# Chunk scan, gated unit and squared-ReLU unit on one core: how C is spread over its heads, what the first tokens are read from, and which steps go first

## Chip, cores and metric

One core of one Trainium2 chip runs the whole program. The metric is device microseconds of one execution; the median over several executions counts. TensorE is PE in the profile, its weight loads PEld, VectorE is DVE, ScalarE is ACT, GpSimd is POOL, and SyncE, whose queue issues the DMAs, is SP.

## The reference

Three stages follow each other, all in float32.

The scan takes 4 batches of 8 heads, 768 tokens each, 32 values per token and head and a state of 16. It is a linear recurrence, written in chunks:

```
L = exp(cum_i - cum_j) for j <= i              # cum: running sum of log(clip(a))
y_intra = ((C B^T) * L) x                      # inside a chunk
y_inter = (C state) * exp(cum)                 # from the chunks before
state   = decay_full * state + sum(decay_from_j * B x)
```

Its 3072 x 256 output goes through a gated unit, `silu(x w_gate) * (x w_val) w_out` with 1536 hidden columns (called GLU below), and that one's output through `relu(x w_in)^2 w_out` with 2048 hidden columns.

## The kernel before, in words

Every operation is put into a graph with an engine, a modelled cost, its dependencies, a priority (a smaller number goes first) and the buffers that it takes. `Graph.order` simulates the engines with these costs and writes out one order for all; each engine then works through its own instructions strictly in that order. So a priority or a modelled cost is not followed at run time, but fixes what stands ahead of what on each queue, SP's DMA issues included.

The scan runs in 28 chunks of up to 112 tokens, seven for each batch (`chunk_ops`). Chunk k needs the state of chunk k-1: the PE product `ys` (L668) gives outputs and state, ACT copies the state out (L702), PE turns it (L707) and ACT puts it into the next chunk's operand (L710). A chunk also needs its decays, scanned on DVE (L600 for chunk 0 and all late chunks, two halves at L570 for chunks 1 to 6), scores on PE (`cb`, L630), and their product on DVE (L654, two per chunk). The seven chunks of batch 0 are the early ones. Their B and C come by DMA: B into `eb` (L461), C into `ec` (L471), a 128 x 4 x 128 tile of zeros into which two DMAs put each head in a place of its own. PE transposes B once (L479) and the four slabs of C (L481), ACT copies both out (L485, L488). A POOL product (L614) makes the state columns; it reads `eb`, and only after it may the DMA of the next but one chunk write there.

Each weight comes as float64 words in units of two DMAs (L379). ACT (L394, L388) and DVE (L400, L405, L409) make float32 of a unit. A split then makes two float32r parts of it, `hi` on ACT (L415) and `lo` on POOL (L420). There are nine units for the GLU (six `gv`, gate and value columns, and three `o`), eight for the last stage.

A GLU step takes one block of 128 hidden columns over some tokens. An exact step multiplies the float32 tokens `xf` with the unconverted unit, two matmuls for each product; a step in parts takes the products of `xh_all`, `xl_all` with `hi`, `lo`, six matmuls each. Gate and value columns are made by PE (L736), then tanh on ACT (L799), two products on DVE (L802, L805), in parts also a copy on ACT (L821) and the rest on POOL (L826), then the output product on PE (L853). Batch 0 has two tiles, 336 and 432 tokens, whose GLU steps are cut into the cells of `PLAN["cells"]` (pair of blocks, first and last chunk, exact or not); the other six tiles run in order, 72 steps. For the early chunks all seven outputs go into `xf` first (L683); two large copies (L723, L726) then make their parts once all chunks of a tile are there. In the GLU the DVE operations have a priority of 3000 less than the rest of their step (a step's is 10000 or more, an early chunk's or unit's below 3600).

The last stage (`relu2`) has 6 tiles of 512 tokens by 16 blocks. Each of the 96 steps has a front of 6 matmuls (L736), ReLU on ACT (L904), a square on DVE (L907), a copy on ACT (L910), a rest on DVE (L914), and a back of 12 matmuls (L926). When a tile is done, ACT copies one half of its sum and DVE the other (L949, L951), and SP stores both (L954).

PSUM has 8 banks here (`ps=8`). Each of the two first GLU tiles holds two for its sums from its first output product to its end.

Of the kernel before, what the change touches and what calls it, by code (L numbers as in the profile page):

```python
# [34 lines left out]
class Graph:  # L35
# [14 lines left out]
    def order(self):  # L50
        for op in self.ops:
            op.wait = len(op.deps)
            for d in op.deps:
                d.next.append(op)
        avail, out, events, now = {}, [], [], 0.0
# [6 lines left out]
        while left:  # L62
            started = True
            while started:
                started = False
                for eng, ops in avail.items():
# [4 lines left out]
                    for op in ops:  # L71
                        if best is not None and op.prio > best.prio:
                            continue
                        need.clear()
                        for b in op.bufs:
                            if not b.taken:
                                need[b.pool] = need.get(b.pool, 0) + 1
                        if op.keep and "ps" in need:
                            need["ps"] += op.keep()
                        if all(self.pools[p] >= k for p, k in need.items()):  # L80
                            best = op
                    if best is None:
                        continue
                    ops.remove(best)
                    for b in best.bufs:
                        if not b.taken:
                            b.taken = True
                            self.pools[b.pool] -= 1
                    best.start = now
# [8 lines left out]
                    heapq.heappush(events, (now + best.cost, seq, 0, best))  # L98
                    started = True
            if not events:  # L100
                raise RuntimeError("the operations wait for each other: " + str(
                    {e: [(o.eng, o.prio, getattr(o.fn, "__qualname__", "")[-30:], [b.pool for b in o.bufs if not b.taken]) for o in v][:6] for e, v in avail.items()}))
            now = events[0][0]
            while events and events[0][0] <= now:
                _, _, kind, op = heapq.heappop(events)
                if kind == 0:
                    busy[op.eng] = None
                    left -= 1
                    for b in op.bufs:
                        b.left -= 1  # L110
                        if not b.left:
                            self.pools[b.pool] += 1
# [14 lines left out]
def kernel(  # L127
# [64 lines left out]
    eb = [const.tile([P, P], F32, name=f"eb{i}") for i in range(NEB)]  # L192
    ec = [const.tile([P, G, P], F32, name=f"ec{i}") for i in range(NEB)]
# [76 lines left out]
    def setup_eb(i):  # L270

        nc.gpsimd.memset(ec[i], 0.0)
        nc.gpsimd.memset(eb[i][0:NS], 0.0)
        v = eb[i][0:NS].rearrange("p (h n) -> p h n", h=H)
# [3 lines left out]
        )  # L278

# [31 lines left out]
    op_eb = [g.add("POOL", 1100, lambda i=i: setup_eb(i), prio=-999 + 10 * i) for i in range(NEB)]  # L311
# [114 lines left out]
    ck = [Chunk() for _ in range(NK)]  # L426

    def chunk_ops(k, prio, after=(), load_after=()):
# [27 lines left out]
        if early:  # L456
            e = Buf(f"eb{k % NEB}")
            c.bt, psb, psc = Buf("tr"), Buf("ps"), Buf("ps")

            def load_b():  # L460
                nc.sync.dma_start(  # L461
                    out=eb[k % NEB][NS : NS + n].rearrange("p (h n) -> p h n", h=H),
                    in_=B[b, :, t : t + n, :].rearrange("h t n -> t h n"),
                )

            def load_c():
                z = ec[k % NEB]
                for u in range(HG):
                    v = z[NS : NS + n, :, u * 64 : u * 64 + 64].rearrange("p w (s n) -> p w s n", s=G)
                    v = bass.AP(v.tensor, v.offset, [list(v.ap[0]), [P + NS, G], [1, NS]])  # L470
                    nc.sync.dma_start(out=v, in_=C[b, u * G : (u + 1) * G, t : t + n, :].rearrange("h t n -> t h n"))  # L471

            lb = dma("SP", 1, 480, 650, load_b, [op_eb[k % NEB], *load_after], ldp, [e])
            lc = dma("SP", 2, 480, 650, load_c, [op_eb[k % NEB], *load_after], ldp, [e])

            def transpose():
                pb = new(psb, [P, P], F32, "trb")
                pc = new(psc, [P, G, P], F32, "trc")
                nc.tensor.transpose(pb, eb[k % NEB], eye)  # L479
                for w in range(G):  # L480
                    nc.tensor.transpose(pc[:, w], ec[k % NEB][:, w], eye)  # L481

            def copy_b():
                c.bt.t = tt = new(c.bt, [P, 1 + G, P], F32, "bct")
                nc.scalar.activation(tt[:, 0], psb.t, AF.Copy)  # L485
# [5 lines left out]
            o = g.add("PE", 800, transpose, [lb, lc, op_eye, before.tr if before else None], prio, [e, psb, psc, c.bt], lat=250)  # L491
            o1 = g.add("ACT", 300, copy_b, [o], prio, [psb, c.bt])
            c.tr = g.add("ACT", 570, copy_c, [o1], prio, [psc, c.bt])
# [118 lines left out]
        def state_columns():  # L612
            v = eb[k % NEB].rearrange("p (h n) -> p h n", h=H) if early else bc[k % NBC][:, 0]
# [65 lines left out]
        if early:  # L679
# [6 lines left out]
        else:  # L686
            def keep_h():
                nc.scalar.activation(xh_all[:, :, dd], yv()[:, :, :n], AF.Copy)

            def keep_l():  # L690
                nc.vector.tensor_tensor(
                    xl_all[:, :, dd], yv()[:, :, :n], xh_all[:, :, dd].bitcast(F32), op=ALU.subtract
                )

            o1 = g.add("ACT", 360, keep_h, [o], prio - 5, [psy])
            c.x = g.add("DVE", 390, keep_l, [o1], prio - 5, [psy])
# [22 lines left out]
    def in_parts(o, n, prio, deps):  # L719
        d = slice(o, o + n)  # L720

        def high():
            nc.scalar.activation(xh_all[:, :, d], xf_buf.t[:, :, d], AF.Copy)  # L723

        def rest():
            nc.vector.tensor_tensor(  # L726
                xl_all[:, :, d], xf_buf.t[:, :, d], xh_all[:, :, d].bitcast(F32), op=ALU.subtract
            )

        h = g.add("ACT", 230 + 1.67 * n, high, deps, prio, [xf_buf])  # L730
        return g.add("DVE", 170 + 2.1 * n, rest, [h], prio, [xf_buf], port=True)


# [11 lines left out]
    W1, W2 = {}, {}  # L745

    def glu(tl, f, o, n, exact, prio, deps, pool_rest=True):
# [60 lines left out]
        a1 = g.add("ACT", 180 + el, tanh, [o1] if wide else [o1, o2], prio, [pg, tb])  # L808
        a2 = g.add("DVE", 160 + 1.04 * n, gate, [a1], prio - 3000, [pg, tb], lat=60)
        a3 = g.add("DVE", 160 + 1.04 * n, times, [a2, o2], prio - 3000, [pg, pv, tb] if wide else [pg, tb])  # L810
# [5 lines left out]
        else:  # L816
# [11 lines left out]
            a4 = g.add("ACT", 200 + el, high, [a3], prio, [tb, pb])  # L828
# [58 lines left out]
    def relu2(i, f, prio, deps):  # L887
# [47 lines left out]
        o1 = g.add("PE", 6 * 232, front, [u.parts, *deps], prio, [ph, u.hi, u.lo], lat=260)  # L935
        o1.keep = lambda: 0 if ab[0].taken else 2
        o = g.add("ACT", 600, relu, [o1], prio, [ph, tb])
        o = g.add("DVE", 690, square, [o], prio - 3000, [tb])
        o = g.add("ACT", 625, high, [o], prio, [tb, pb])
        o = g.add("DVE" if late else "POOL", 690 if late else 1300, rest, [o], prio - (3000 if late else 0), [tb, pb])  # L940
        bk = g.add("PE", 12 * 120, back, [o], prio, [*ab, pb, u.hi, u.lo], lat=260)
        if f == NF2 - 1:
            for m in range(2):
                ob = Buf("tmp")

                def drain(m=m, ob=ob):
                    ov = new(ob, [P, 512], F32, "o")
                    if m == 0:
                        nc.scalar.activation(ov, acc[-1 - i][m], AF.Copy)  # L949
                    else:  # L950
                        nc.vector.tensor_copy(ov, acc[-1 - i][m])  # L951

                def store(m=m, ob=ob):
                    nc.sync.dma_start(  # L954
                        out=out[t0 + m * 256 : t0 + (m + 1) * 256, :].rearrange("(i p) f -> p i f", p=P),
                        in_=ob.t.rearrange("p (i f) -> p i f", i=2),
                    )

                o = g.add("ACT" if m == 0 else "DVE", 690, drain, [bk], prio - 3000, [ab[m], ob])
                dma("SP", 1, 480, 700, store, [o], prio, [ob])  # L960
# [16 lines left out]
    for u, at in zip(units, PLAN["split_at"]):  # L977
        W1[u].split(abs(at) * 100, "POOL", [last_unit] if at < 0 else [])
    xparts = [
        in_parts(o, n, at * 100, [ck[k].xf for k in ks])  # L980
        for (o, n, ks), at in zip(((0, cut, range(3)), (cut, S - cut, range(3, NCB))), PLAN["xparts_at"])
    ]
    for i, (j, c0, c1, exact) in enumerate(PLAN["cells"]):
        ti, o = (0, c0 * Q) if c0 < 3 else (1, c0 * Q - cut)
        n = min(c1 * Q, S) - c0 * Q
        for f in (2 * j, 2 * j + 1):
            deps = [ck[k].xf for k in range(c0, c1)] if exact else [xparts[ti]]
# [51 lines left out]
    with tc.manual_schedule():  # L1039
# [10 lines left out]
    xparts_at=[0.1, 5.59],  # L1050
    cells=[
        (0, 3, 7, 0),
        (2, 1, 3, 1),
        (3, 3, 7, 0),
        (0, 0, 3, 0),
        (2, 0, 1, 1),
        (2, 3, 7, 0),
        (4, 3, 7, 0),
        (5, 0, 3, 0),
        (3, 0, 3, 1),  # L1060
        (5, 3, 7, 0),
        (1, 5, 7, 1),
        (1, 3, 5, 0),
        (4, 0, 3, 0),
        (1, 0, 3, 0),
    ],
    pace=[-3, 2.73, 1],
    second=[52, 4, 6],
# [31 lines left out]
```

## Time and profile before

| | before |
|---|---|
| median of 3 runs | 692.1 us (690.78 to 692.5) |
| profiled execution | 690.22 us |
| span of its trace | 688.4 us |
| PE busy | 643.6 us, 93% of the span |
| DVE busy | 414.9 us, 60% |
| ACT busy | 328.2 us, 48% |
| POOL busy | 230.5 us, 33% |
| mean granted TensorE clock | 0.984 |

The span runs from the first to the last instruction; the profiled execution took 1.8 us more than that, and the median of the runs lies 1.9 us above the profiled execution. A stretch's idle time of an engine is its length less the busy time. The granted clock is a share of 2.4 GHz.

### The profile page before, as it was taken

The page shows a single profiled execution, that of the slowest core. Times are in us where ns is not written, and L with a number is a line of the kernel's source. Part 1 is how long each engine was busy: PE and PEld are TensorE (multiplying, and loading weights), DVE is VectorE, ACT ScalarE, POOL GpSimd, SP SyncE. Part 2 cuts the span into 40 slices and gives each one's busy share as a digit, 9 for nine tenths or more (in the row PEclk, how much of TensorE's full clock was granted, in tenths as well). Part 3 has the DMA queues.
Part 4 walks back from the last instruction along what each step waited for, and adds up shares of the span by engine and source line. Part 5 has one row for each costly group of instructions (what it writes and reads, how often), then busy time and mean ns, then how long its engine had stood idle before and what let it go on. Part 6 is the DMA issues. An engine that isn't in the chain of part 4 may idle for free.

```text
span 688.4 us, 11170 instructions
## 1 busy us (share of the span) xinstructions
PE 643.6 (93%) x4339; PEld 583.0 (85%) x4339; DVE 414.9 (60%) x588; ACT 328.2 (48%) x641; POOL 230.5 (33%) x228
## 2 busy tenths in 40 slices
PE   2567999999999999999999998999999999999996
PEld 1455788999998899888999977898989999998985
DVE  6999965347666664756566797545363535353533
ACT  6467454244454544544556664435353534343432
POOL 5244667336756654566355571000000000000000
PEclk9986999999999999999999999999999999999998
DMA  7768721504565576643432310000000000000000
GB/s 229 179 163 203 151 63 44 98 2 78 105 136 107 80 129 119 134 73 69 153 106 80 119 65 1 0 31 1 1 32 1 3 29 1 31 1 1 31 0 31
DMA packets 135829, 49.55 MB, mean 72 GB/s; under 512 B 121216, under 2 KB 124288, under 8 KB 135776
## 3 DMA queue, kind: packets, MB, share of 16 engines
q1 hardware_dynamic: 135776, 48.84, 30.5%
q8 instruction: 34, 0.56, 0.3%
q14 instruction: 19, 0.16, 0.1%
HBM read 34.59 MB, written 3.22 MB: 55 GB/s over the span
## 4 chain that ended last, share of the span: by engine, by line
PE 83%; DVE 8%; issue 2%; ACT 2%; DMA 2%; POOL 1%; SPq 1%; ACTq 0%; DVEq 0%; POOLq 0%
PE acc L926 20%; PE h L736 18%; PE g L736 14%; PE acc L853 13%; PE v L736 13%; PE ys L668 2%; DVE v L409 2%; DVE raw L400 2%; DVE v L405 1%; DMA ec<-in_C_dram 1%; PE cb L639 1%; ACT raw L394 1%; DMA raw<-in_moe_w_val_dram 1%; PE turn L707 1%; POOL p L826 1%
## 5 line engine op out<-in xcount | busy, mean ns | idle before, releaser
L926 PE MATMUL acc<-hi,p 128*128 128x256 f32 x768 | 142.8, 284 | 5.8 <-DVE p L914 3.0
L907 DVE TENSOR_TENSOR t<-t 128x512 f32<-128x512 f32 x96 | 68.2, 714 | 132.2 <-ACT t L904 130.4
L826 POOL TENSOR_TENSOR p<-t,p 128x432 fp32r<-128x432 f32 (+2 forms) x92 | 102.2, 1115 | 92.2 <-ACT p L821 89.8
L926 PEld LDWEIGHTS acc<-hi,p 128*128 128x128 f32 x768 | 121.6, 192 | 8.0 <-ACT p L910 3.6
L904 ACT ACTIVATE t<-h 128x512 f32<-128x512 f32 x96 | 57.2, 597 | 147.4 <-PE h L736 130.3
L926 PE MATMUL acc<-lo,p 128*128 128x256 f32 x384 | 108.8, 283 | 0.0
L802 DVE SCALAR_TENSOR_TENSOR t<-t,g 128x336 f32<-128x336 f32 (+4 forms) x100 | 53.3, 533 | 77.4 <-ACT t L799 76.7
L853 PE MATMUL acc<-p,hi 128*128 128x432 f32 (+2 forms) x368 | 97.5, 344 | 2.3 <-POOL p L826 2.2
L821 ACT ACTIVATE p<-t 128x432 fp32r<-128x432 f32 (+2 forms) x92 | 47.7, 520 | 66.5 <-DVE t L805 66.1
L799 ACT ACTIVATE t<-g 128x336 f32<-128x336 f32 (+4 forms) x100 | 47.4, 475 | 65.7 <-PE g L736 59.9
L736 PE MATMUL h<-xh_all,lo 128*128 128x512 f32 x192 | 76.0, 396 | 0.0
L736 PE MATMUL h<-xl_all,hi 128*128 128x512 f32 x192 | 75.8, 395 | 0.0
L736 PE MATMUL h<-xh_all,hi 128*128 128x512 f32 x192 | 75.7, 394 | 0.0
L926 PEld LDWEIGHTS acc<-lo,p 128*128 128x128 f32 x384 | 73.6, 192 | 1.1
L853 PEld LDWEIGHTS acc<-p,hi 128*128 128x128 f32 x368 | 64.8, 188 | 7.5 <-POOL p L826 4.6
L914 DVE TENSOR_TENSOR p<-t,p 128x512 fp32r<-128x512 f32 x96 | 65.7, 686 | 4.5 <-ACT p L910 4.3
L736 PE MATMUL g<-xh_all,hi 128*128 128x432 f32 (+2 forms) x188 | 65.1, 346 | 0.0
L910 ACT ACTIVATE p<-t 128x512 fp32r<-128x512 f32 x96 | 60.1, 627 | 10.2 <-PE acc L926 6.7
L736 PE MATMUL g<-xl_all,hi 128*128 128x432 f32 (+2 forms) x188 | 63.1, 336 | 0.1
L736 PE MATMUL g<-xh_all,lo 128*128 128x432 f32 (+2 forms) x188 | 62.9, 335 | 0.0
L736 PE MATMUL v<-xh_all,hi 128*128 128x432 f32 (+1 forms) x180 | 62.4, 346 | 0.0
L853 PE MATMUL acc<-p,lo 128*128 128x432 f32 (+2 forms) x184 | 62.0, 337 | 0.0
(99 smaller groups left out, 1142.9 us busy)
## 6 DMA issues: line engine op xcount, KB each, us to landing
ab<-decay SPq DMA_DIRECT2D x21, 452.0 KB, 4.6
raw<-in_moe_w_out_dram SPq DMA_DIRECT2D x14, 512.0 KB, 5.1
raw<-in_moe_w_in_dram SPq DMA_DIRECT2D x8, 512.0 KB, 3.6
raw<-in_moe_w_gate_dram SPq DMA_DIRECT2D x6, 512.0 KB, 3.6
raw<-in_moe_w_val_dram SPq DMA_DIRECT2D x6, 512.0 KB, 4.8
out_dram<-o SPq DMA_DIRECT2D x12, 256.0 KB, 2.1
xa<-in_x_dram SPq DMA_DIRECT2D x24, 112.0 KB, 2.7
bc<-in_B_dram SPq DMA_DIRECT2D x18, 56.0 KB, 3.2
```

Of the source, the lines that this page charges most:

```text
L400: nc.vector.scalar_tensor_tensor(low, high, 0x80000000, low, op0=ALU.bitwise_and, op1=ALU.bitwise_or)
L736: nc.tensor.matmul(ps, l, r, start=(i == 0), stop=(i == len(terms) - 1))
L799: nc.scalar.activation(t[:, :n], gg(), AF.Tanh, scale=0.5)
L802: nc.vector.scalar_tensor_tensor(tb.t[:, :n], tb.t[:, :n], 1.0, gg(), op0=ALU.add, op1=ALU.mult)
L821: nc.scalar.activation(p[:, 0, :n], tb.t[:, :n], AF.Copy)
L826: e.tensor_tensor(p[:, 1, :n], tb.t[:, :n], p[:, 0, :n].bitcast(F32), op=ALU.subtract)
L853: nc.tensor.matmul(ps, l, r, start=bank not in done_f, stop=f == NF - 1, skip_group_check=True,)
L904: nc.scalar.activation(new(tb, [P, TN], F32, "t"), ph.t, AF.Relu)
L907: nc.vector.tensor_tensor(tb.t, tb.t, tb.t, op=ALU.mult)
L910: nc.scalar.activation(new(pb, [P, 2, TN], F32R, "p")[:, 0, :], tb.t, AF.Copy)
L914: e.tensor_tensor(pb.t[:, 1, :], tb.t, pb.t[:, 0, :].bitcast(F32), op=ALU.subtract)
L926: nc.tensor.matmul(ps, pb.t[:, l, tk], r, start=(f == 0 and s == 0 and q % 2 == 0), stop=(f == NF2 - 1 and s == 2), skip_group_check=True,)
```

## The change

C goes the way of B: one DMA into the second half of a tile `eb`, now 128 x 2 x 128, and one transpose. The four copies that lie one behind the other in the operand of the scores are then made by ACT from the one transposed C, each with a scale that is one for the rows of one head of each group and zero for the others; POOL makes this `mask` once. `ec` is gone, and so is the second PSUM bank of the transposes.

Every early chunk now makes its parts `xh_all` and `xl_all` from PSUM, as late chunks did; the large copies of `in_parts` are gone. `xf` is still kept for the chunks in exact cells, which are all seven.

`PLAN` is another: chunks, units, splits and cells have another order, and 7 of 15 cells are exact instead of 4 of 14. The loads of late chunks may start 8 steps ahead instead of 1, and the units 4 to 7 of the last stage 6 steps sooner. GLU and ReLU steps have a priority of 30000 less on DVE, and on ACT as well. A front of the last stage has 25 less than before, which is two and a half steps. The last tile's sums are drained in four pieces, two by ACT and two by DVE, and ACT's are stored from ACT's queue.

The model counts an operation of DVE and one of POOL that use the shared port as one after the other, in both directions.

```diff
-                    if best.port and eng == "DVE":
-                        o = busy.get("POOL")
+                    if best.port and eng in ("DVE", "POOL"):
+                        o = busy.get("POOL" if eng == "DVE" else "DVE")
                         if o and o.port:
-                            best.cost += 0.6 * min(o.start + o.cost - now, best.cost)
+                            best.took += o.start + o.took - now
...
+    def setup_mask():
+        nc.gpsimd.memset(mask2, 1.0)
+        for sign, base in ((1, 0), (-1, NS - 1)):
+            nc.gpsimd.affine_select(
+                out=mask2, in_=mask2, pattern=[[-sign * G * NS, HG], [-sign * NS, G]], base=base,
+                channel_multiplier=sign, compare_op=ALU.is_ge, fill=0.0,
+            )
+        nc.gpsimd.tensor_tensor(mask, mask2[:, 0], mask2[:, 1], op=ALU.add)
...
-            lc = dma("SP", 2, 480, 650, load_c, [op_eb[k % NEB], *load_after], ldp, [e])
+            lc = dma("SP", 1, 480, 650, lambda: load_b(1, C), [op_eb[k % NEB], *load_after], ldp, [e])
             def transpose():
-                pb = new(psb, [P, P], F32, "trb")
-                pc = new(psc, [P, G, P], F32, "trc")
-                nc.tensor.transpose(pb, eb[k % NEB], eye)
-                for w in range(G):
-                    nc.tensor.transpose(pc[:, w], ec[k % NEB][:, w], eye)
+                pb = new(psb, [P, 2, P], F32, "trb")
+                for i in range(2):
+                    nc.tensor.transpose(pb[:, i], eb[k % NEB][:, i], eye)
...
             def copy_c():
-                nc.scalar.activation(c.bt.t[:, 1:, NS : NS + n], psc.t[:, :, NS : NS + n], AF.Copy)
+                for w in range(G):
+                    nc.scalar.activation(
+                        c.bt.t[:, 1 + w, NS : NS + n], psb.t[:, 1, NS : NS + n], AF.Copy, scale=mask[:, w : w + 1]
+                    )
...
-        if early:
+        if k in need_f:
             def keep_f():
...
-        else:
-            def keep_h():
+        def keep_h():
+            nc.scalar.activation(xh_all[:, :, dd], yv()[:, :, :n], AF.Copy)
+        def keep_l():
+            nc.vector.tensor_tensor(
+                xl_all[:, :, dd], yv()[:, :, :n], xh_all[:, :, dd].bitcast(F32), op=ALU.subtract
+            )
...
-        a1 = g.add("ACT", 180 + el, tanh, [o1] if wide else [o1, o2], prio, [pg, tb])
-        a2 = g.add("DVE", 160 + 1.04 * n, gate, [a1], prio - 3000, [pg, tb], lat=60)
+        a1 = g.add("ACT", 180 + el, tanh, [o1] if wide else [o1, o2], prio - GATE_A, [pg, tb])
+        a2 = g.add("DVE", 160 + 1.04 * n, gate, [a1], prio - GATE, [pg, tb], lat=60)
...
-        o1 = g.add("PE", 6 * 232, front, [u.parts, *deps], prio, [ph, u.hi, u.lo], lat=260)
+        o1 = g.add("PE", 6 * 232, front, [u.parts, *deps], prio - 10 * PLAN["lead"], [ph, u.hi, u.lo], lat=260)
...
+            cuts = 2 if i == T // TN - 1 else 1
             for m in range(2):
...
+                        q = nc.scalar if by_act and cuts == 2 else nc.sync
...
-    chunk_at=[9.12, 0.42, 7.01, 3.77, 19.09, 0.3, 16.6],
-    unit_at=[2.09, 6.28, 0, 4.92, 4.03, 11.18, 17.82, 10.45, 16.95],
-    split_at=[-35.23, 23.48, 19.42, 32.86, 18.17, -19.9, 21.31, 16.46, 21.5],
+    chunk_at=[3.7, 5.0, 15.8, 3.2, 0, 8.2, 7.9],
+    unit_at=[0, 0, 6.4, 6.9, 8.0, 32.7, 22.4, 16.5, 28.4],
+    split_at=[-3.8, 0.1, 20.7, 24.1, 6.9, -0.2, 13.3, -4.6, -31.1],
     cells=[
-        (0, 3, 7, 0), (2, 1, 3, 1), (3, 3, 7, 0), (0, 0, 3, 0), (2, 0, 1, 1), (2, 3, 7, 0), (4, 3, 7, 0),
-        (5, 0, 3, 0), (3, 0, 3, 1), (5, 3, 7, 0), (1, 5, 7, 1), (1, 3, 5, 0), (4, 0, 3, 0), (1, 0, 3, 0),
+        (2, 2, 3, 1), (1, 3, 7, 1), (0, 3, 7, 1), (3, 0, 2, 1), (3, 2, 3, 1), (2, 0, 2, 0), (0, 1, 3, 0), (2, 3, 7, 0),
+        (3, 3, 7, 0), (0, 0, 1, 1), (5, 0, 3, 0), (4, 0, 3, 0), (1, 0, 3, 1), (4, 3, 7, 0), (5, 3, 7, 0),
     ],
-    pace=[-3, 2.73, 1],
-    second=[52, 4, 6],
+    pace=[-3, 2.85, 8],
+    second=[53, 4, 0],
+    gate=[30000, 30000],
+    lead=2.5,
```

## Rows read from the trace of the kernel before

**Rows 1.** Busy time by stretch: PE, PEld, DVE, ACT, POOL, granted clock, DMA share, GB/s

```profile
30.00:60.00 30.00, 16.27 (x166) 12.77 (x164) 29.90 (x30) 19.05 (x34) 12.49 (x8) 0.75 0.65 175
60.00:90.00 30.00, 28.43 (x208) 23.49 (x205) 25.73 (x35) 15.63 (x33) 18.35 (x16) 0.96 0.79 171
...
250.00:400.00 150.00, 148.29 (x998) 138.52 (x998) 98.44 (x143) 80.15 (x164) 82.50 (x76) 1.00 0.42 102
400.00:450.00 50.00, 45.91 (x277) 40.25 (x277) 35.09 (x42) 26.13 (x42) 13.87 (x6) 1.00 0.06 22
450.00:680.00 230.00, 229.84 (x1461) 208.12 (x1460) 108.30 (x165) 93.56 (x166) 0.00 (x0) 1.00 0.04 12
680.00:689.00 9.00, 2.40 (x12) 1.90 (x12) 2.07 (x3) 1.76 (x3) 0.00 (x0) 0.69 0.17 58
```

**Rows 2.** The same view cut at the first GLU output product

```profile
0.00:67.50 67.50, 35.22 (x344) 27.11 (x344) 58.45 (x66) 42.35 (x73) 28.00 (x45) 0.87 0.76 191
67.50:120.00 52.50, 51.90 (x340) 45.10 (x341) 36.78 (x53) 25.57 (x57) 34.62 (x31) 1.00 0.41 89
```

**Rows 3.** Timeline, batch 0: start us, us, engine line op out<-in xcount

```profile
28.46 1.21 DVE L409 SCALAR_TENSOR_TENSOR v<-v,raw 128x1024 uint32<-128x1024 uint32 x1
...
29.59 0.69 DVE L405 TENSOR_SCALAR v<-v 128x1024 f32<-128x1024 f32 x1
...
30.19 1.22 DVE L400 SCALAR_TENSOR_TENSOR raw<-raw 128x1024 uint32<-128x1024 uint32 x1
...
30.84 2.76 POOL L420 TENSOR_TENSOR lo<-v,hi 128x1024 fp32r<-128x1024 f32 x1 [4.77 <-ACT hi L415]
...
31.44 3.24 DVE L409 SCALAR_TENSOR_TENSOR v<-v,raw 128x1024 uint32<-128x1024 uint32 x1
...
38.33 0.27 ACT L799 ACTIVATE t<-g 128x112 f32<-128x112 f32 x1
...
50.80 0.54 ACT L488 ACTIVATE bct<-trc 128x448 f32<-128x448 f32 x1
...
65.62 1.02 DVE L654 TENSOR_TENSOR mt<-cb,L 128x384 f32<-128x384 f32 x2
...
67.27 0.26 DVE L802 SCALAR_TENSOR_TENSOR t<-t,g 128x112 f32<-128x112 f32 x1
...
67.50 0.99 PE L853 MATMUL acc<-t,v 128*128 128x224 f32 x4 [0.38 <-DVE t L805]
...
69.84 1.04 PE L853 MATMUL acc<-t,v 128*128 128x112 f32 x8
...
73.99 0.50 DVE L802 SCALAR_TENSOR_TENSOR t<-t,g 128x336 f32<-128x336 f32 x1
...
82.45 0.38 DVE L691 TENSOR_TENSOR xl_all<-ys,xh_all 128x224 fp32r<-128x224 f32 x1
```

**Rows 4.** Chain that ended last: start us, us, engine line; six matmuls in parts, four exact records

```profile
95.05 0.92 PE g L736 x6
...
97.82 1.18 PE g L736 x6
...
106.05 1.13 PE g L736 x4
```

**Rows 5.** What PE (columns as in rows 3) and DVE did from 414 us on

```profile
414.32 4.04 DVE L907 TENSOR_TENSOR t<-t 128x512 f32<-128x512 f32 x3
...
419.02 0.50 PE L926 MATMUL acc<-hi,p 128*128 128x256 f32 x2 [2.80 <-DVE p L914]
```

**Rows 6.** Timeline at the end, columns as in rows 3

```profile
679.94 0.60 ACT L904 ACTIVATE t<-h 128x512 f32<-128x512 f32 x1 [5.15 <-PE h L736]
...
681.98 0.39 PE L926 MATMUL acc<-hi,p 128*128 128x256 f32 x1 [2.13 <-ACT p L910]
...
682.70 0.50 PE L926 MATMUL acc<-hi,p 128*128 128x256 f32 x2 [0.22 <-DVE p L914]
...
684.64 0.69 DVE L951 COPY o<-acc 128x512 f32<-128x512 f32 x1 [1.99 <-PE acc L926]
```

More of the change, by code (lines that the diff above doesn't have):

```diff
@@ L54, in order @@
                 d.next.append(op)
+        free = {p: [None] * n for p, n in self.pools.items()}
         avail, out, events, now = {}, [], [], 0.0
@@ L79, in order @@
                             need["ps"] += op.keep()
-                        if all(self.pools[p] >= k for p, k in need.items()):
+                        if all(len(free[p]) >= k for p, k in need.items()):
                             best = op
@@ L87, in order @@
                             b.taken = True
-                            self.pools[b.pool] -= 1
-                    best.start = now
+                            best.after.append(free[b.pool].pop(0))
+                    best.start, best.took = now, best.cost
                     out.append(best)
                     busy[eng] = best
-                    if best.port and eng == "DVE":
-                        o = busy.get("POOL")
+                    if best.port and eng in ("DVE", "POOL"):
+                        o = busy.get("POOL" if eng == "DVE" else "DVE")
                         if o and o.port:
-                            best.cost += 0.6 * min(o.start + o.cost - now, best.cost)
+                            best.took += o.start + o.took - now
                     seq += 1
-                    heapq.heappush(events, (now + best.cost, seq, 0, best))
+                    heapq.heappush(events, (now + best.took, seq, 0, best))
                     started = True
             if not events:
-                raise RuntimeError("the operations wait for each other: " + str(
-                    {e: [(o.eng, o.prio, getattr(o.fn, "__qualname__", "")[-30:], [b.pool for b in o.bufs if not b.taken]) for o in v][:6] for e, v in avail.items()}))
+                raise RuntimeError("the operations wait for each other")
             now = events[0][0]
@@ L310 @@
     op_eye = g.add("POOL", 550, setup_pool, prio=-1000)
-    op_eb = [g.add("POOL", 1100, lambda i=i: setup_eb(i), prio=-999 + 10 * i) for i in range(NEB)]
+    op_eb = [g.add("POOL", 350, lambda i=i: setup_eb(i), prio=-999.5 + 0.1 * i) for i in range(NEB)]
+    op_mask = g.add("POOL", 600, setup_mask, prio=-999)
     op_delta = g.add("POOL", 2000, setup_delta, prio=-998)
@@ L426 @@
     ck = [Chunk() for _ in range(NK)]
+    need_f = {k for _, c0, c1, exact in PLAN["cells"] if exact for k in range(c0, c1)}
     def chunk_ops(k, prio, after=(), load_after=()):
@@ L934, in relu2 @@
         ab = accbuf[-1 - i]
-        o1 = g.add("PE", 6 * 232, front, [u.parts, *deps], prio, [ph, u.hi, u.lo], lat=260)
+        o1 = g.add("PE", 6 * 232, front, [u.parts, *deps], prio - 10 * PLAN["lead"], [ph, u.hi, u.lo], lat=260)
         o1.keep = lambda: 0 if ab[0].taken else 2
[L937 to L940, printed above, removed]
+        o = g.add("ACT", 600, relu, [o1], prio - GATE_A, [ph, tb])
@@ L941, in relu2 @@
+        o = g.add("DVE", 690, square, [o], prio - GATE, [tb], port=True)
+        o = g.add("ACT", 625, high, [o], prio - GATE_A, [tb, pb])
+        o = g.add("DVE", 690, rest, [o], prio - GATE, [tb, pb], port=True)
         bk = g.add("PE", 12 * 120, back, [o], prio, [*ab, pb, u.hi, u.lo], lat=260)
         if f == NF2 - 1:
+            cuts = 2 if i == T // TN - 1 else 1
             for m in range(2):
[L944 to L960, printed above, removed]
+                for c in range(cuts):
+                    ob = Buf("tmp")
+                    by_act = (m if cuts == 1 else c) == 0
+                    w = 512 // cuts
+                    def drain(m=m, ob=ob, by_act=by_act, cs=slice(c * w, c * w + w)):
+                        ov = new(ob, [P, 512], F32, "o")[:, : w]
+                        if by_act:
+                            nc.scalar.activation(ov, acc[-1 - i][m][:, cs], AF.Copy)
+                        else:
+                            nc.vector.tensor_copy(ov, acc[-1 - i][m][:, cs])
+                    def store(ob=ob, by_act=by_act, r0=t0 + m * 256 + c * (w // 2)):
+                        q = nc.scalar if by_act and cuts == 2 else nc.sync
+                        q.dma_start(
+                            out=out[r0 : r0 + w // 2, :].rearrange("(i p) f -> p i f", p=P),
+                            in_=ob.t[:, :w].rearrange("p (i f) -> p i f", f=256),
+                        )
+                    o = g.add("ACT" if by_act else "DVE", 690 // cuts, drain, [bk], prio - GATE, [ab[m], ob])
+                    dma("ACT" if by_act and cuts == 2 else "SP", 1, 480, 700, store, [o], prio, [ob])
@@ L986 @@
         for f in (2 * j, 2 * j + 1):
-            deps = [ck[k].xf for k in range(c0, c1)] if exact else [xparts[ti]]
+            deps = [ck[k].xf if exact else ck[k].x for k in range(c0, c1)]
             glu(tiles[ti], f, o, n, exact, 10000 + i * 10, deps)
```

89 lines of the change are left out of this document (33 added, 56 removed).

## Prediction, made before the changed kernel ran

> **What bounds the kernel now.** I read the busy times by stretch first, then the timeline of batch 0, the chain that ended last for prices, and the ends of the trace. From 67.5 us on PE hardly ever stops: it is idle for 0.6 us up to 120 us [rows 2], 1.7 us from 250 to 400, 4.1 us from 400 to 450 and 0.2 us from 450 to 680 [rows 1]. Before 67.5 us it is busy for 35.2 us and idle for 32.3 [rows 2]. At the end it works for 2.4 of the last 8.4 us [rows 1]. So the time is PE's work plus three holes: the start (32.3), the passage from the GLU to the last stage (4.1) and the tail (6.0).
>
> The hole at the start belongs to DVE, which is busy for 58.5 of the first 67.5 us and 29.9 of those from 30 to 60 [rows 1, 2]. It makes units and scans there while PE waits. The timeline shows two further things. A tanh of a GLU step is done at 38.6 us, yet the first gate product of that shape starts at 67.27 [rows 3], although such a product takes 0.26 us: in DVE's order every chunk and unit stood ahead of it. And the last step of a unit takes 1.21 us alone but 3.24 us when it starts 0.6 us into a 2.76 us POOL split [rows 3]: it waits out POOL's instruction and then runs.
>
> **The change part by part.** All sums are made against the profiled execution's 690.22 us.
>
> *Start, what DVE must do before chunk 6.* Before, eight of nine units are through DVE when the last early chunk's products end at 66.64 us (start 65.62, 1.02 us) [rows 3]. In the new plan the priorities of gv3, gv4 and gv5 (2840 and more, 2240) and of o2 (1650) put them behind the chunks (a chunk waits for the one before it, so chunks 2 to 6 sit at 1580). So five units stand ahead of chunk 6, three fewer: 3 x (1.22 + 0.69 + 1.21) = 9.4 us off DVE [rows 3]. Of the collisions with POOL, 2.03 us each by the two rows of that step, I count 1.5 fewer (-3.0 us), since five of nine splits now stand late. Added: six of the small rests that take 0.38 us (2.3 us), and the gates of the steps that now come early. These steps are: gv0 on chunk 0 and gv2 on chunk 2, each 2 blocks x 2 products x 0.26 = 1.0 us, and gv1 on chunks 0 to 2, 2 x 2 x 0.50 = 2.0 us [rows 3]; with 0.6 for a product or two already there before, +3.5. Together -9.4 - 3.0 + 2.3 + 3.5 = -6.6, so the products of chunk 6 end at 60.0 us. `ys` and `xf` follow before and after alike.
>
> *Start, what PE has done by then.* Before, 24 exact records by 67.5 us: 16 of the 112-token cells and 8 of 224 tokens. At full clock a 112-token record takes 1.04/8 = 0.13 us [rows 3]; a 336-token one 1.13/4 = 0.28 [rows 4], from which I estimate 0.19 for 224. That is 2.1 + 1.5 = 3.6 us. After: a step has 12 exact records, so gv0 on chunk 0 and gv2 on chunk 2 are 2 x 12 x 0.13 = 3.1 us each and gv1 on chunks 0 to 2 is 2 x 12 x 0.28 = 6.8, together 13.0 us. I take all of it as done by 60.9 us (0.9 after the products, the distance that 67.5 has to 66.64): PE has some 25 idle us to put it in.
>
> *What more PE must do.* Exact steps cost more. Per step in parts of 18 matmuls: 432 tokens 3 x 1.18 = 3.54 us, 336 tokens 3 x 0.92 = 2.76 [rows 4]. For 224 tokens I take 2.1 us, an estimate: in proportion 1.84, but not below what 18 weight loads need, and the exact 112-token record shows 0.13 us for one load with little to stream, so 18 x 0.13 = 2.3 is the other end. Exact: 336 tokens 3 x 1.13 = 3.39, 432 in proportion 4.36, 208 in proportion 2.10, 112 tokens 1.56. The new cells have one 432 and two 336 fewer in parts, one 224 more, two exact 432 more, one exact 208 fewer and two exact 112 more: -3.54 - 5.52 + 2.1 + 8.72 - 2.10 + 3.12 = +2.8 us for each of the two blocks, 5.6 us in all. It is PE's own time and nothing hides it.
>
> *After that point* PE needs 28 us of exact and early parts cells while DVE makes the deferred units and gates (4 x 3.12 = 12.5 us, and about 10 for sixteen or so products of 0.5 to 0.7). The stretch from 400 to 450, where units are also made between steps, left PE idle for 4.1 us; I allow half of this, 2 us, against 0.6 before.
>
> Start in sum: (67.5 - 60.9) + (13.0 - 3.6) - 5.6 - 1.4 = **9.0 us less**.
>
> *C by one transpose and four scaled copies.* ACT's one copy of 448 columns at 0.54 us [rows 3] becomes four of 112. No scaled copy is in the trace; the nearest row is the 112-column tanh, also from PSUM, at 0.27, so 4 x 0.27 = 1.1 us at most, and 0.54 if they overlap fully: 0 to 0.55 us more per chunk, 0 to 3.9 over seven. ACT is busy for 19 of 30 us in that stretch [rows 1], and the copies of the next chunk lie beside the scans of this one, so I take nothing; if DVE didn't cover it, all 3.9 would be on the chunks' path. A bank and three transposes go, one DMA issue per chunk too; all stand in PE's and SP's idle time, and I take nothing. Parts straight from PSUM put one more ACT copy ahead of the state's copy in each chunk, as wide as the rest of 0.38 us. That chain, too, waits for DVE: nothing, with up to 7 x 0.38 = 2.7 us if it doesn't. POOL's setup loses the clearing of `ec` and gains the mask, all small beside the 2.76 us of its 1024-column row, while it is busy for 28.0 of 67.5 us [rows 2]: nothing, at most 1 us either way.
>
> *Gates first* also means that ACT and DVE, which work in order, stand still when a step's front is late, with units and the chunks' copies queued behind a tanh, and late chunks behind gates. DVE has 51.6 of the 150 us from 250 to 400 free [rows 1], so the late chunks cost nothing there; without this cover the 1.7 us of PE's waits in that stretch could double.
>
> *Passage, 400 to 450 us.* PE waits 2.80 us for the rest on DVE [rows 5]; DVE's three squares there took 4.04 us, 1.35 each, twice the 0.69 of a copy as wide [rows 5, 6], while POOL still splits: it is busy for 13.87 us of the stretch [rows 1]. These units may now start 6 steps (some 20 us) sooner, and steps go before units on DVE and ACT. What is late next is the GLU's own tail. I take 2 of the 4.1 us as gone, with 3.5 less and 2 more (units starved by the gates until the passage, one more collision) as the ends.
>
> *Tail.* The last front ends just before 679.94, then its four steps follow, and PE waits 2.13 and 0.22 us [rows 6]. With fronts two and a half steps ahead the last front comes before the two backs ahead of it, which cover the chain (682.70 - 679.94 = 2.8 us against two backs of about 1.4 us: 1461 matmuls in 230 us at 18 a step [rows 1] are 2.83 us a step, half of it the back): 2.35 us gone. The drain that ends last falls from 0.69 to half of it, 0.35 less [rows 6]. Sum 2.7, ends 0.3 (fronts can't run ahead) and 4 (the granted clock, 0.69 on average in that stretch and so partly at 1.2 GHz, after PE's wait [rows 1], stays at 2.4 as well).
>
> ACT and DVE now drain halves of one bank, where each had a bank of its own; the row for it is a 0.69 us drain that starts alone [rows 6]. The Trainium skill (PSUM — Partial Sum Buffer, section on bank collisions) says that two engines must not touch the same bank and quadrant at one time, reads included. By this rule the halves go one after the other and the 0.35 us are lost again: 2.35 in place of 2.7. No row of this trace shows it.
>
> Sum: 9.0 + 2.0 + 2.7 = 13.7 us. 690.22 - 13.7 = 676.5 for an execution like the profiled one; the median lies 1.9 above that one, so 692.1 - 13.7 = 678.4 us.
>
> **Rivals.**
>
> *1. Slower: PSUM banks tie chunks to GLU steps.* Before, the first output product, which takes banks for the sums, came at 67.50, behind all early chunks [rows 3]. Now the two tiles hold 4 of 8 banks while the chunks run, and a chunk's two scan banks and two score banks must share the rest with gate and value columns. If each of chunks 3 to 6 waits for one step of gv1 on chunks 0 to 2 (fronts 2.3, tanh, two products at 0.50, about 4 us), the end of chunk 6 moves from 60 by 16 us. Each microsecond costs one, so the start loses 7 and the whole is 692.1 + 7 - 4.7 = 694.4 us. It decides from 73.7 us on for the end of chunk 6 (60 + 13.7). Against it: one transposition bank fewer, and from 67.5 to 120 us PE ran late chunks beside both tiles' sums with 0.6 us idle [rows 2].
>
> *2. The start's gain is eaten.* Chunk 6 ends at 67 us, because the units' removal from DVE is replaced by chunk latency (DMA, POOL's state columns, the longer ACT copies), and exact steps cost their 5.6: start 2.0, with the rest 6.7, time 685.4. For it: 16.3 us of PE's 30 to 60 were at a granted clock of 0.75 [rows 1], so chunk work there isn't short. Against: DVE had 0.1 us idle there.
>
> *3. More.* All collisions before chunk 6 go (another 3.1 us), gv2 is split early so that its parts cell on chunks 0 and 1 (4.2 us) is done too, no bubbles (2.0), passage 3.5: 678.4 - 10.8 = 667.6.
>
> *4. No change in effect.* The chip's order doesn't follow the model, the start stands as it was with 5.6 more PE work, and passage and tail give 4.7: 693.0.
>
> **How the numbers follow.** Forecast 0.50, rival 1 0.09, rival 2 0.22, rival 3 0.14, rival 4 0.05. The range runs from 668 (nearly rival 3) to 690 (above rival 2): it leaves out a third of rival 3 and rivals 1 and 4, 0.19 in all. The likeliest case's own range is 672 to 684, from the ends of its terms. A difference of 0.3%, 2.1 us, is what can be told from no change. Of rivals 1 and 4 (0.14) 0.10 count as slower and 0.04 as same; of the others 0.03 may end within the bound. Faster 0.83, same 0.07, slower 0.10.
>
> **What would show it.** Right: the first GLU output product before 35 us and gates within 2 us of their tanh; PE saturated from about 61 us; the sum of the exact cells' PE time 5.6 us higher; no 2 us wait before the last back; less than 2.5 us idle from 400 to 450. Wrong: products of chunk 6 later than 67 us, PE waiting for `gv` units between 60 and 100 us, or idle time between 90 and 400 that wasn't there.

## The result and the profile after

The changed kernel takes 674.74 us (median, 674.5 to 675.3) against 691.44 us before, a ratio of 0.976 with a 95% interval of 0.974 to 0.978. The forecast was 678.4 us, its range 668 to 690. The profiled execution took 675.3 us with a span of 673.6 us, 14.8 us less than the span before.

Busy time by stretch of the changed kernel, in the columns of rows 1 (PE, PEld, DVE, ACT, POOL, granted clock, DMA share, GB/s):

```profile
0.00:30.00 30.00, 11.13 (x103) 8.48 (x104) 21.63 (x31) 19.22 (x39) 12.09 (x34) 1.00 0.83 199
30.00:60.00 30.00, 25.93 (x286) 21.74 (x285) 28.40 (x43) 22.43 (x60) 14.57 (x13) 0.89 0.78 174
60.00:90.00 30.00, 27.16 (x116) 16.40 (x117) 26.87 (x32) 14.12 (x25) 11.14 (x8) 1.00 0.71 154
90.00:250.00 160.00, 159.01 (x1137) 145.57 (x1136) 97.53 (x153) 77.54 (x185) 93.09 (x96) 1.00 0.52 96
250.00:385.00 135.00, 134.63 (x901) 126.22 (x900) 87.71 (x125) 71.61 (x145) 77.86 (x69) 1.00 0.40 95
385.00:435.00 50.00, 50.00 (x299) 45.67 (x299) 39.06 (x49) 28.81 (x45) 15.36 (x8) 1.00 0.14 43
```

From 30 to 60 us PE is busy for 25.9 us instead of 16.3 [rows 1], with DVE nearly as busy (28.4 against 29.9), and at a granted clock of 0.89 instead of 0.75. The passage to the last stage, 385 to 435 us here, has no idle time left; before, it had 4.1 us [rows 1].

The timeline of the changed kernel, columns as in rows 3:

```profile
28.71 0.26 DVE L796 SCALAR_TENSOR_TENSOR t<-t,g 128x112 f32<-128x112 f32 x1
...
29.43 0.67 PE L847 MATMUL acc<-t,v 128*128 128x112 f32 x4 [0.81 <-DVE t L799]
...
57.42 1.01 DVE L662 TENSOR_TENSOR mt<-cb,L 128x384 f32<-128x384 f32 x2
...
74.78 1.14 ACT L406 ACTIVATE raw<-raw 128x1024 int32<-128x1024 uint16 x1 [4.06 <-DMA raw<-in_moe_w_val_dram]
...
76.36 0.60 DVE L796 SCALAR_TENSOR_TENSOR t<-t,g 128x432 f32<-128x432 f32 x1 [2.30 <-ACT t L793]
...
77.73 1.72 PE L847 MATMUL acc<-t,v 128*128 128x432 f32 x4 [1.61 <-DVE t L799]
```

The first gate product stands at 28.7 us, not at 67.3, the first output product at 29.4 and not at 67.5, and chunk 6's products end at 58.4 us, not at 66.6 [rows 3]. The last three lines are one of the waits that are new. PE waits 1.61 us for a gate product, DVE had stood for 2.30 us until the tanh before it, and ACT, which works in order, had stood for 4.06 us until the DMA of a deferred unit landed, with that tanh behind it.

ACT's copies that close a GLU tile give the lead at the end of batch 0. First the kernel before, then the changed one:

```profile
143.92 0.95 ACT L875 ACTIVATE xh_all<-acc 128x432 fp32r<-128x432 f32 x2
154.34 0.77 ACT L875 ACTIVATE xh_all<-acc 128x336 fp32r<-128x336 f32 x2
```

```profile
133.29 0.91 ACT L869 ACTIVATE xh_all<-acc 128x336 fp32r<-128x336 f32 x2 [0.18 <-PE acc L847]
146.31 0.93 ACT L869 ACTIVATE xh_all<-acc 128x432 fp32r<-128x432 f32 x2
```

The later of the two tiles closes 8.0 us sooner (146.31 against 154.34), with as many matmuls of PE done by then but for the 21 transposes that the change saves (898 against 919). So much the start gave. The rest of the 14.8 us is the passage (4.1), the tail (2.0, below) and some 0.7 between.

### The profile page after: what moved, and what is told of

Its sections match the earlier page's. It is cut to its first block, busy times and chain, and to the rows that moved or that the text cites. A ratio compares the mean times of both kernels' runs of the same rounds, so it can differ in the third digit from the quotient of the medians.

```text
span 673.6 us, 11146 instructions
## 1 busy us (share of the span) xinstructions
PE 641.3 (95%) x4318; PEld 575.9 (85%) x4318; DVE 418.6 (62%) x598; ACT 337.7 (50%) x666; POOL 224.1 (33%) x226
## 4 chain that ended last, share of the span: by engine, by line
PE 88%; DMA 4%; POOL 3%; ACT 2%; DVE 1%; SPq 1%; issue 1%; DVEq 0%; ACTq 0%; POOLq 0%
PE acc L920 20%; PE h L729 20%; PE g L729 15%; PE acc L847 14%; PE v L729 13%; PE ys L676 2%; POOL p L820 2%; DMA raw<-in_moe_w_val_dram 2%; PE cb L647 1%; DMA eb<-in_B_dram 1%; POOL lo L432 1%; PE cb L638 1%; DMA bct<-bcs 1%; PE turn L715 1%; ACT raw L406 1%
## 5 line engine op out<-in xcount | busy, mean ns | idle before, releaser
L920 PE MATMUL acc<-hi,p 128*128 128x256 f32 x768 | 152.5, 283 | 0.0
L920 PEld LDWEIGHTS acc<-hi,p 128*128 128x128 f32 x768 | 125.5, 191 | 4.0
L901 DVE TENSOR_TENSOR t<-t 128x512 f32<-128x512 f32 x96 | 69.8, 728 | 70.5 <-ACT t L898 70.4
L796 DVE SCALAR_TENSOR_TENSOR t<-t,g 128x432 f32<-128x432 f32 (+3 forms) x102 | 53.4, 524 | 64.3 <-ACT t L793 63.6
L847 PE MATMUL acc<-p,hi 128*128 128x432 f32 (+2 forms) x352 | 92.2, 342 | 1.0 <-POOL p L820 0.9
L793 ACT ACTIVATE t<-g 128x432 f32<-128x432 f32 (+3 forms) x102 | 47.7, 469 | 58.2 <-PE g L729 56.3
L815 ACT ACTIVATE p<-t 128x432 fp32r<-128x432 f32 (+2 forms) x88 | 45.6, 519 | 60.9 <-DVE t L799 59.2
L847 PEld LDWEIGHTS acc<-p,hi 128*128 128x128 f32 x352 | 61.9, 188 | 6.1 <-POOL p L820 2.4
L799 DVE SCALAR_TENSOR_TENSOR t<-t,v 128x432 f32<-128x432 f32 (+1 forms) x90 | 50.1, 557 | 26.0 <-PE v L729 19.6
L432 POOL TENSOR_TENSOR lo<-v,hi 128x1024 fp32r<-128x1024 f32 x17 | 45.0, 2650 | 45.7 <-ACT hi L427 43.0
```

Of the source, the lines that this page charges most:

```text
L432: e.tensor_tensor(self.lo.t, self.v.t, self.hi.t.bitcast(F32), op=ALU.subtract)
L793: nc.scalar.activation(t[:, :n], gg(), AF.Tanh, scale=0.5)
L796: nc.vector.scalar_tensor_tensor(tb.t[:, :n], tb.t[:, :n], 1.0, gg(), op0=ALU.add, op1=ALU.mult)
L799: nc.vector.scalar_tensor_tensor(tb.t[:, :n], tb.t[:, :n], 0.5, vv(), op0=ALU.mult, op1=ALU.mult)
L847: nc.tensor.matmul(ps, l, r, start=bank not in done_f, stop=f == NF - 1, skip_group_check=True,)
L901: nc.vector.tensor_tensor(tb.t, tb.t, tb.t, op=ALU.mult)
```

## Experiments

**The tail's four pieces.** In the changed kernel the last piece's copy waits for a DMA. Its tail (L949 and L951 are the drains on ACT and DVE, L955 the stores):

```profile
667.85 0.39 ACT L949 ACTIVATE o<-acc 128x256 f32<-128x256 f32 x1 [1.62 <-PE acc L920]
...
668.26 0.42 DVE L951 COPY o<-acc 128x256 f32<-128x256 f32 x1 [1.31 <-ACT o L949]
668.50 0.38 ACT L949 ACTIVATE o<-acc 128x256 f32<-128x256 f32 x1 [0.27 <-PE acc L920]
...
670.38 0.42 DVE L951 COPY o<-acc 128x256 f32<-128x256 f32 x1 [1.69 <-DMA out_dram<-o]
```

The pool `tmp` has three buffers, and the fourth piece must wait until a store has left one. Two kernels tell what this costs.

```diff
-            cuts = 2 if i == T // TN - 1 else 1
+            cuts = 1
```

> The changed kernel with the last tile's sums drained in two pieces, one by ACT and one by DVE, both stored from SP, as before. In the changed kernel's trace the fourth piece's copy waits 1.69 us for a store to finish, since its pool has three buffers; with two pieces nothing waits, and from the end of the last back to the end of the span it takes 3.8 us as before instead of 5.1: 673.4 us. If four pieces are worth the 0.35 us that the prediction gave them, 675.1 us.

```diff
-                    ob = Buf("tmp")
+                    ob = Buf("p" if m and not (c == 0) else "tmp") if cuts == 2 else Buf("tmp")
```

> The changed kernel with the fourth piece of the last tile put into a buffer of another pool, so that it doesn't wait for a store. If the wait of 1.69 us is that of the buffer, the last copy starts at about 668.8 instead of 670.4 us of the span and the end comes 1.5 us sooner: 673.2 us. If the two engines' reads of one bank are what holds it (one after the other), the copy of 0.4 us still queues and 0.4 of this is lost: 673.6. If the stores themselves set the end: 674.7.

One cut: 673.61 us, ratio 0.974 (0.972 to 0.975). A fourth buffer: 674.08 us, ratio 0.975 (0.974 to 0.976). Both medians are below 674.74, but all three intervals overlap, so no faster version is proved. The traces decide: with the fourth buffer the last copy starts right behind ACT's.

```profile
667.54 0.38 ACT L949 ACTIVATE o<-acc 128x256 f32<-128x256 f32 x1 [0.27 <-PE acc L920]
...
667.96 0.42 DVE L951 COPY o<-acc 128x256 f32<-128x256 f32 x1 [0.23 <-ACT o L949]
```

From the last back's end to the span's end it is 4.0 us there (667.52 to 671.5), 4.0 with one cut (667.95 to 672.0) and 5.1 in the changed kernel (668.48 to 673.6). So the wait was the buffer's and costs 1.1 us; four pieces are worth nothing over two. Both DVE copies start behind ACT's copy of the other half of the same bank, so cutting each bank between the two engines gained nothing. By the rule of the Trainium skill (PSUM — Partial Sum Buffer, bank collisions) that the prediction weighed, two engines are to be kept off one bank. The trace agrees: 667.96 us behind 667.54 + 0.38.

**Lead.**

```diff
-    lead=2.5,
+    lead=0,
```

> The changed kernel with fronts of the last stage at their own priority (lead 0 instead of 2.5). If the lead is what covers the last step's four operations, PE waits again for 2.1 to 2.4 us before the last back: 676.9 us, and 0.7 more if the clock falls in that wait: 677.6. If gates first already let the fronts run ahead, 674.7.

675.27 us, ratio 0.976 (0.975 to 0.978): not to be told from the changed kernel. The chains show why, first the kernel before, then the changed one, then this one:

```profile
672.69 5.75 PE acc L926 x48
678.44 1.42 PE h L736 x6
682.70 1.91 PE acc L926 x10
```

```profile
662.74 1.40 PE h L729 x6
664.15 4.33 PE acc L920 x36
```

```profile
647.09 5.60 PE h L729 x24
652.70 5.76 PE acc L920 x48
658.45 1.42 PE h L729 x6
...
663.27 4.36 PE acc L920 x34
```

In the changed kernel the last front has two other backs between itself and its own, as forecast. Without the lead PE works in groups of four fronts and four backs, as it did before. Before, the last group was a single front, behind which nothing lay; here it is three fronts and three backs, and the other two cover most of the last one's chain (PE waits 0.3 us). So the lead covers the chain, but with the rest of this plan the groups would have covered it too, and its worth can't be told from nothing. What made the groups fall differently wasn't tried.

**Gates.** Late again in the changed kernel, and first in the kernel before (there in all steps' operations on ACT and DVE, of which one stands here):

```diff
-    gate=[30000, 30000],
+    gate=[3000, 0],
```

> The changed kernel with the priorities of the GLU and ReLU steps as before (3000 less on DVE, none less on ACT); all else as changed. If gates first fill the hole at the start (first gate product at 28.7 us instead of 66.6), most of the start's gain goes, some 6 to 8 us, and the passage waits again for 2 to 4: 682 to 686 us. If instead the new order of units, chunks and cells makes the gain, within 1.5 us of 674.7.

```diff
-        a2 = g.add("DVE", 160 + 1.04 * n, gate, [a1], prio - 3000, [pg, tb], lat=60)
+        a2 = g.add("DVE", 160 + 1.04 * n, gate, [a1], prio - 30000, [pg, tb], lat=60)
...
```

> The kernel before with one part of the change alone: tanh and the copy on ACT, and the products and rests on DVE, of GLU and ReLU steps have 30000 less. If gates first alone makes the gain, the steps that PE has already begun at 35 to 65 us go on, the passage no longer waits (4.1 us), and the time is 681 to 684 us. If gates first only pays with units and cells put in an order that leaves exact steps to do early, the start keeps its hole and only the passage gains: 687 to 689 us.

Late gates: 707.7 us, ratio 1.023 (1.022 to 1.025), slower than the kernel before by 16 us and far more than either theory had. Gates first alone: 684.7 us, ratio 0.990 (0.988 to 0.992), 7 us of the 16.7. In the kernel with late gates the first tanh is done at 33.6 us (27.6 in the changed kernel), but the products come at 60 to 67 us once more (tanh on ACT, then the product of that shape on DVE):

```profile
33.33 0.24 ACT L793 ACTIVATE t<-g 128x112 f32<-128x112 f32 x1
```

```profile
59.61 0.26 DVE L796 SCALAR_TENSOR_TENSOR t<-t,g 128x112 f32<-128x112 f32 x1
...
65.89 0.26 DVE L796 SCALAR_TENSOR_TENSOR t<-t,g 128x112 f32<-128x112 f32 x1
```

The passage to the last stage waits again as well, 7.9 us from 390 to 450 us, in the columns of rows 1:

```profile
390.00:450.00 60.00, 52.13 (x265) 47.32 (x266) 40.93 (x48) 30.96 (x47) 27.63 (x15) 0.91 0.10 36
```

So gates that wait cost the plan its gain and more. How much more can't be said exactly, since each of these kernels also has a newly drawn order: late gates cost 33 us against the changed kernel, and the orders drawn anew below cost 13.6 to 18.6 us with the gates first.

**The order of before, C's old way, large copies.** Three parts taken back, each with a new order drawn by the planner: chunks, units, splits and cells as before; C's loads, bank, transposes, copy and their costs as before; `in_parts` as before.

```diff
-    chunk_at=[3.7, 5.0, 15.8, 3.2, 0, 8.2, 7.9],
+    chunk_at=[9.12, 0.42, 7.01, 3.77, 19.09, 0.3, 16.6],
...
```

> The changed kernel with the order of chunks, units, splits and cells of before (4 exact cells of 14); gates first, C by one transpose, parts from PSUM, pace and lead as changed. If the deferred units and the early exact cells are worth what the prediction gave them, the start loses 4 to 6 us: 679 to 681 us. If the other parts make the gain, 675 us or less, since the exact cells' 5.6 us of PE work go.

```diff
-                    nc.tensor.transpose(pb[:, i], eb[k % NEB][:, i], eye)
+                    nc.tensor.transpose(pc[:, w], ec[k % NEB][:, w], eye)
...
```

> The changed kernel with C as before: two DMAs into a tile of zeros, four transposes of C into a PSUM bank of their own, one copy on ACT. If C's way is off the path at the start, as the prediction has it, 674 to 676 us. If the bank, the DMA issues and the PE transposes in its place matter while chunks and steps share 8 banks, each chunk from the second on is later by 0.5 to 1 us: 678 to 681.

```diff
-            deps = [ck[k].xf if exact else ck[k].x for k in range(c0, c1)]
+            deps = [ck[k].xf for k in range(c0, c1)] if exact else [xparts[ti]]
```

> The changed kernel with the parts of the early tokens made from xf by one large copy and one large rest for each of the two tiles, as before, so that cells in parts wait for all chunks of their tile. The only cell in parts that can run early is gv2 on chunks 0 and 1 (4.2 us of PE work); if that early cell fills an idle stretch, it is lost there and comes back later: 677 to 680 us. If PE has enough exact cells by then, 674 to 676.

692.18, 693.33 and 692.77 us, with ratios of 1.001 (0.999 to 1.002), 1.002 (1.000 to 1.003) and 1.002 (1.000 to 1.003): each loses the whole gain, and no theory had 692 to 693 for any of them. A single wait shows what happened with the large copies: PE stood for 10.3 us behind one product of a late chunk, with exact steps queued behind it. POOL made that chunk's state columns only at 82.62 us, since DVE's scan before them ended at 82.47.

```profile
PE ys L676 <- POOL mt L622: 10.7, 2, 10.3
```

**The order itself.** If any new order loses the gain, then so does one that was drawn for no reason. Two numbers of the model, and nothing that is computed:

```diff
-            o1 = g.add("ACT", 260, copy_b, [o], prio, [psb, c.bt])
+            o1 = g.add("ACT", 300, copy_b, [o], prio, [psb, c.bt])
```

> The changed kernel with one number of the planner's model changed: the copy of the transposed B counts 300 ns instead of 260. Every instruction is there as before, but 482 lines of DVE's order differ. If the start's gain hangs on the one order for which the plan's priorities were set, and undoing C's way or the parts from PSUM lost it by drawing another order, this loses much of it as well, though nothing is added: 680 to 694 us. If those parts are worth their 18 us by themselves, this stays within 2 us of 674.7.

```diff
-            c.tr = g.add("ACT", 1480, copy_c, [o1, op_mask], prio, [psb, c.bt])
+            c.tr = g.add("ACT", 1040, copy_c, [o1, op_mask], prio, [psb, c.bt])
```

> The changed kernel with the model's cost of the four scaled copies at 1040 ns, which is what they took in the changed kernel's trace, instead of 1480; nothing else. If the order is fragile, 680 to 694 us though the model is nearer to the chip; if a better model gives as good an order, 673 to 676 us.

692.18 us, ratio 1.002 (1.001 to 1.004), and 688.30 us, ratio 0.996 (0.995 to 0.997). The first, 40 ns of the model, costs 17.4 us, the second 13.6. In the trace of the first, which is of an execution of 695.52 us, 3.3 above its median:

```profile
60.00:65.00 5.00, 2.36 (x12) 1.85 (x12) 4.97 (x9) 3.76 (x9) 4.06 (x2) 0.83 0.96 164
65.00:70.00 5.00, 5.00 (x27) 3.37 (x27) 4.57 (x5) 2.81 (x7) 4.08 (x3) 0.50 0.77 143
```

```profile
62.79 0.39 PE L715 MATMUL turn<-eye,st 128*16 128x128 f32 x2 [1.50 <-ACT st L710]
...
67.50 2.95 PE L729 MATMUL g<-xf,v 128*128 128x432 f32 x4
...
71.74 1.61 PE L729 MATMUL g<-xf,v 128*128 128x432 f32 x4
...
80.28 0.85 PE L647 MATMUL cb<-bct 128*128 128x112 bf16 x8 [2.96 <-DMA bct<-bcs]
```

PE has 41.1 us idle in this span (693.8 less 652.7 busy) against 32.3 (673.6 less 641.3), and is busy for 11.4 us more with the same work. Much of the second part is the clock: after the stretch with 2.6 us idle of 5 it is granted 0.50 for 5 us, and the four records of an exact product of 432 tokens take 2.95 us instead of 1.61. The mean granted clocks allow at most some 7.7 of the 11.4 us for it, an estimate (0.016 x 693.8 less 0.005 x 673.6); the rest stays open. Here waits were paid twice, once as idle time and once at 1.2 GHz. Not every wait is: the 2.8 us from 60 to 90 us in the changed kernel left the clock at 1.00.

The end of chunk 6 isn't what was lost. Its products end earlier than in the changed kernel (58.4 us) in three of the kernels that lose the gain, at 58.1 us with 1040 ns, at 57.5 with the large copies and at 54.1 with late gates. First the run with 1040 ns, then late gates:

```profile
57.15 0.99 DVE L662 TENSOR_TENSOR mt<-cb,L 128x384 f32<-128x384 f32 x2
```

```profile
53.07 1.02 DVE L662 TENSOR_TENSOR mt<-cb,L 128x384 f32<-128x384 f32 x2
```

What they lose comes behind it: from 60 to 90 us PE is idle for 6.9, 12.4 and 7.7 us, against 2.8 in the changed kernel, and the later tile closes at 158.8, 162.8 and 163.6 us, against 146.3.

**C's way in the changed kernel's own order.** The clean form of the experiment keeps the model's costs and buffers as for the new way, so that every queue's order stays, and changes only what the operations do (the diff is against the run with C's old way above). Its other side doubles ACT's copies in the same order.

```diff
-            o = g.add("PE", 800, transpose, [lb, lc, op_eye, before.tr if before else None], prio, [e, psb, psc, c.bt], lat=250)
+            o = g.add("PE", 300, transpose, [lb, lc, op_eye, before.tr if before else None], prio, [e, psb, c.bt], lat=250)
...
```

> The changed kernel with C's old way (two DMAs into a tile of zeros, four transposes into a bank of their own, one wide copy), but with the model's costs and buffers as for the new way, so that every engine's order is the changed kernel's. If C's way by itself is worth little and the 693.3 us of the run that also drew a new order came from that order, 674 to 679 us. If the old way itself costs the gain, 688 us or more.

```diff
-                for w in range(G):
+                for w in (0, 0, 1, 1, 2, 2, 3, 3):
```

> The changed kernel in its own order on every engine, with each of the four scaled copies of C made twice: 1.0 us more of ACT for each of the seven early chunks. If ACT's copies are off the path at the start, as the prediction has it, 674 to 676 us. If the chunks' chain runs through them, up to 7 us more: 681.

678.05 us, ratio 0.981 (0.979 to 0.983), and 679.51 us, ratio 0.983 (0.981 to 0.985). So C's new way is worth 3.3 us by itself, and 15.3 of the 18.6 us that its undoing had cost came from the other order. The plan of before and the large copies weren't repeated in the changed kernel's order, so what they are worth by themselves stays open. The doubled copies cost 4.8 us: four took 1.04 to 1.09 us in the changed kernel, so seven times this, 7.4 us of ACT's time, came through to two thirds.

```profile
29.54 1.04 ACT L494 ACTIVATE bct<-trb,mask 128x112 f32<-128x112 f32 x4
```

## Why the prediction was right, point by point

- *DVE's hole and chunk 6.* Forecast 60.0 us for the end of its products, measured 58.4. That gates behind chunks and units waste the steps begun early was confirmed by the late gates (707.7 us). That the end of chunk 6 carries the start's gain was not: three kernels with an earlier end lost 13.6 to 33 us.
- *PE's work by then.* Forecast 13.0 us, of gv0 on chunk 0, gv2 on chunk 2 and gv1 on chunks 0 to 2. By 60.9 us the trace has the first two (48 records at 0.13, 6.2 us), 8 of 24 records of gv1 (2.2) and, not expected in the likeliest case, gv2 on chunks 0 and 1 in parts (36 matmuls, 4.2 us by the prediction's price): 12.6 us.
- *More PE work.* The prices held: an exact product of 432 tokens starts 1.45 us after the one before it (67.33, 68.78 us), as estimated. The sum of 5.6 us can't be read by itself, since PE's busy time also changed with the better clock and with 21 transposes fewer, from 643.6 to 641.3 us.
- *After that point.* 2 us of waits allowed; measured 2.8 from 60 to 90 us, and 1.0 up to 250. Other orders raise this term, up to 12.4 us from 60 to 90 us, and half of an idle time from another stage was a thin ground for it. Start in sum: 9.0 forecast, 8.0 measured where batch 0 closes.
- *C's way* was put at nothing with 0 to 3.9 us more as its range for the copies. This step failed: it saves 3.3 us. The copies do lie on the chunks' path (4.8 us when doubled), and the old way's one copy is the shorter one (0.54 us [rows 3] against 1.04); what it has more of are transposes, DMAs, a bank of PSUM and POOL's clearing of `ec`. In the same order it has 21 matmuls more (4339 against 4318), PE is busy for 2.6 us more (643.9 against 641.3) and idle for 0.5 more, which points to the transposes. No run tried these parts one by one.
- *Passage.* Forecast 2.0, measured 4.1, the term that was most undersized. It stays free of idle time in the kernels that have the changed kernel's gates, pace and units of the last stage, whatever became of their start: from 390 to 450 us PE is busy for 60.00 us with before's plan, with C's old way, with the large copies and with both changes of the model. With late gates it waits for 7.9 us, and gates first alone left 2.6: by these two runs the gates are needed and don't do it alone. Which of the others takes the rest wasn't tried.
- *Tail.* Forecast 2.7, measured 2.0. With three backs and one front still to do it took 12.8 us before (2.9 us of backs ahead of the last front's start at 678.44) and 10.9 now (from 662.74). The wait of 2.35 us went; the drain, put at 0.35 less, became 1.3 longer, 1.1 of it by the buffer that had been overlooked. The lead does what was forecast of it, but isn't needed: without it the time is the same.
- *Rivals.* PSUM banks (1) didn't bind: chunk 6 ended before 60 us although the sums' banks were taken from 29.4 us. Early parts cells, part of rival 3, came true. That chunk 6 ends at 67 us with the gain eaten (rival 2) didn't come. A start with no gain at all (rival 4, there because the chip wouldn't follow the model) was given 0.05; it is what an order drawn with another 40 ns in the model gives, by another cause. The prediction took the order for a property of the change and not of one draw, and had no term for this. Its sum was right for the order that was drawn. In that order it was lucky, for nothing in the working singled it out, and of the five others above with the gates first, each with one part or one number changed, none kept more than 3.1 us of the gain.

## What to carry to other kernels

When a planner writes out the order, the unit of change is the order: compare two versions of a part only in the same order, by keeping the model's costs and buffers and changing what the operation does, and take a few draws with slightly changed costs before a gain is put down to a part. On an engine that works in order, put the operations on which the bounding engine waits ahead of those that only prepare later work; here, beginning steps early without that came out worse than the kernel before (707.7 us). Count the buffers of every pool that a finer cut draws on.

## What the runs showed of the hardware

Waits of PE in the start stage can cost more than their length: with the same matmuls PE's busy time ran from 641.3 us (granted clock 0.995) to 652.7 (0.984), in part because the clock fell to 1.2 GHz after stretches in which PE had waited. Four ACT copies of 128 x 112 from PSUM in a row, each with a scale by partition, took 1.04 to 1.09 us in the changed kernel, 0.26 to 0.27 each, as long as a single tanh of that shape without such a scale (0.24 to 0.27). A single copy's record is longer, 0.32 to 0.37 us, and the records of a row overlap.
